# Attention and feed-forward on one core: two layer-one blocks to a bank, joined attention runs, a shorter state update

## The chip, the cores and the metric

The kernel runs on one core of a Trainium2 chip. The metric is the device time of one execution in microseconds, as the median of several runs. The profile is one execution; its span (first to last instruction) is 1.7 to 1.9 us shorter than the timed figure.

## The reference

Per batch and head, a gated linear attention: a 48 x 48 state decays by `alpha` at each of 768 steps, takes up the product of `k` and `v`, and is read by `q`. Its output, 3072 tokens of 384 features, goes through two dense layers with a tanh-gelu between.

```python
batch, n_heads, seq, head_dim = (4, 8, 768, 48)
for t in range(S):
    state = alpha[:, :, t, :, None] * state + einsum('bhd,bhe->bhde', k[:, :, t], v[:, :, t])
    y[:, :, t] = einsum('bhd,bhde->bhe', q[:, :, t], state)
x = y.transpose(0, 2, 1, 3).reshape(B * S, H * D)          # 3072 x 384
h = x @ w_in                                               # 384 -> 2048
g = 0.5 * h * (1 + tanh(c * (h + 0.044715 * h**3)))
out = g @ w_out                                            # 2048 -> 384
```

## The kernel before

The sequence is cut into six chunks of 128 tokens. A *unit* is one batch in one chunk, with eight heads; a *pair* is two units, and there are twelve pairs (0 to 11). For a pair, ACT forms exponentials of cumulative sums of log(alpha), DVE multiplies them into q and k (`qp`, `kp`), TensorE or a DMA turns these, TensorE forms the attention products `at` (k against q, 64 rows for each head), DVE masks them (`atm`), and TensorE forms y from them and from the state. y, turned, is the input of the two dense layers: layer one (`hT`), gelu on ACT (`gT`), layer two (`acc`). A small scheduler in the program, with a table of estimated costs `W`, decides the order in which all of this is recorded; on each engine the order is then fixed.

The eight accumulator banks of PSUM are given to three tags: `ca` (one buffer of two banks: cumulative sums, and one unit's attention products), `yk` (two of one bank), and `ff` (four of one bank: layer one, layer two, and in places attention products).

```python
BUFS = dict(ca=1, yk=2, ff=4, ...)

def attn(self, u, i):                       # one unit: 8 products of 64-row tiles
    ...
        if (u["m"], i) in self.AT_FF:
            at = [self.tile("ff", [C, H // 2, C], F32, "at") for _ in range(2)]
        else:
            at = self.tile("ca", [C, 2, H // 2, C], F32, "at")
            at = [at[:, 0], at[:, 1]]
        for p in range(H // 2):
            for o in range(2):
                sl = slice(64 * o, 64 * o + 64)
                nc.tensor.matmul(at[o][:, p, :], t[sl, 1, p, :], t[sl, 0, p, :], start=True, stop=True)

def carry(self, u, i, c, b):                # the state: four DVE operations of 64 partitions
    ...
        for o in range(2):
            ps, fs = slice(64 * o, 64 * o + 64), slice(D * o, D * o + D)
            acc = kv[ps, :, fs]
            if c > 0:
                s = self.sb.tile([C, H // 2, D], F32, tag=f"stmp{o}", bufs=2, name="stmp")
                nc.vector.tensor_tensor(s[ps], acc, old[ps, :, fs], op=ALU.add)
                acc = s[ps]
            nc.vector.tensor_tensor(new[ps, :, fs], acc, u["bend"][ps, i, :, None].to_broadcast(...), op=ALU.mult)

def layer1(self, f, c, lo, hi, nt):         # one block of 128 features for 256 tokens: half a bank
    ...
        h = f["h", c, lo, nt] = self.tile("ff", [self.C, (hi - lo) * self.C], F32, "hT")
        for j in range(self.NKT):           # 3 matmuls
            self.nc.tensor.matmul(h, ...)
def gelu(self, f, c, lo, hi, nt):           # one gelu a block
    ...
# ... (loads, exponentials, turns, y, layer two and the scheduler are cut)
```

Of the kernel before, what the change touches and what calls it, by code (L numbers as in the profile page):

```python
# [17 lines left out]
    qk2=910, qk1=500, ev8=650, ev4=350, mask=640, st=1400, st0=700, xc=520, xe=330, ot=540,  # L18
# [118 lines left out]
class _Kernel:  # L137
# [16 lines left out]
    AT_FF = ((0, 1),)  # L154

    URGENT = (2,)
    BUFS = dict(ca=1, yk=2, ff=4, la=3, qp=4, kp=4, b8=2, kn=2, qkT=4, atm=6, x=3, ot=6, bend=8,
                a=4, q=4, k=4, v=6)

    def __init__(self, ctx, tc, q, k, v, alpha, w_in, w_out, out):  # L160
# [25 lines left out]
        self.w_out = const.tile([C, self.NFT, self.d_model], BF16, name="w_out")  # L186
        self.state = [[const.tile([C, H // 2, 2 * D], BF16, name=f"st{b}_{i}") for i in range(2)]
# [222 lines left out]
    def attn(self, u, i):  # L410
        nc, H, C = self.nc, self.H, self.C

        def emit(e):
            t = u["T"][:, :, i]
            if (u["m"], i) in self.AT_FF:
                at = [self.tile("ff", [C, H // 2, C], F32, "at") for _ in range(2)]
            else:
                at = self.tile("ca", [C, 2, H // 2, C], F32, "at")
                at = [at[:, 0], at[:, 1]]
            u["at", i] = at  # L420
            for p in range(H // 2):
                for o in range(2):
                    sl = slice(64 * o, 64 * o + 64)
                    nc.tensor.matmul(at[o][:, p, :], t[sl, 1, p, :], t[sl, 0, p, :], start=True, stop=True)  # L424
        return emit
# [19 lines left out]

    def carry(self, u, i, c, b):
        nc, H, C, D = self.nc, self.H, self.C, self.D

        def emit(e):
            kv, old, new = u["kv", i], self.state[b][c % 2], self.state[b][(c + 1) % 2]  # L450
            for o in range(2):
                ps, fs = slice(64 * o, 64 * o + 64), slice(D * o, D * o + D)
                acc = kv[ps, :, fs]
                if c > 0:
                    s = self.sb.tile([C, H // 2, D], F32, tag=f"stmp{o}", bufs=2, name="stmp")
                    nc.vector.tensor_tensor(s[ps], acc, old[ps, :, fs], op=ALU.add)  # L456
                    acc = s[ps]
                nc.vector.tensor_tensor(new[ps, :, fs], acc,  # L458
                                        u["bend"][ps, i, :, None].to_broadcast([64, H // 2, D]), op=ALU.mult)
        return emit  # L460
# [32 lines left out]
    def layer1(self, f, c, lo, hi, nt):  # L493
        def emit(e):
            h = f["h", c, lo, nt] = self.tile("ff", [self.C, (hi - lo) * self.C], F32, "hT")
            for j in range(self.NKT):
                self.nc.tensor.matmul(h, self.w_in[:, j, nt * self.C:(nt + 1) * self.C],  # L497
                                      self.xT[c][:, j, lo:hi].rearrange("p g t -> p (g t)"),
                                      start=j == 0, stop=j == self.NKT - 1)
        return emit  # L500

    def gelu(self, f, c, lo, hi, nt):
        return lambda e: self.nc.scalar.activation(  # L503
            self.gT[c % self.NG][:, nt, lo * self.C:hi * self.C], f.pop(("h", c, lo, nt)), AF.Gelu_apprx_tanh)
# [32 lines left out]
    def tasks(self):  # L537
# [57 lines left out]
        for m, (c, i) in enumerate(pairs):  # L595
# [4 lines left out]
            lns[m], ends[m], qp, kp, be = [], [], [None, None], [None, None], [None, None]  # L600
            cums, exps = [], []
            for lo, hi in self.parts(m):
# [8 lines left out]
                if u["sums"]:  # L611
                    be[lo:hi] = [x[2]] * n
# [19 lines left out]
            vs, kvs, tq, cs, users = [], [], [], [], []  # L632
# [3 lines left out]
            if u["packed"]:  # L636
# [7 lines left out]
                owner = every[0]  # L644
            for j in range(2):
                b, o = 2 * i + j, P + 10 + 3 * j
                k = kp[j]
# [16 lines left out]
                at = s.add("attn", {"PE": W["attn"]}, o + 1, self.attn(u, j), turned)  # L664
                ms = [s.add("mask", {"DVE": W["mask"]}, o + 2, self.mask(u, j, h), [at]) for h in range(2)]
                if (m, j) in self.AT_FF:
                    at.take("ff", ms[0]).take("ff", ms[1])
                else:
                    at.take("ca", *ms)
# [12 lines left out]
                ats.setdefault(m, []).append(at)  # L682
# [3 lines left out]
                if c < NCH - 1:  # L686
                    if u["packed"]:
# [7 lines left out]
                                              [kv, be[j]] + ([states[b, c - 1], ys[b, c - 1]] if c else []))  # L695
# [12 lines left out]
            owner.take("qkT", *users)  # L708
# [3 lines left out]
            if u["sums"]:  # L712
                be[0].take("bend", *cs)


        n = 0
# [3 lines left out]
        def layer1(m):  # L720
# [4 lines left out]
            size = str(hi - lo)  # L725
            for nt in range(self.NFT):
                t = s.add("l1", {"PE": W["l1_" + size]}, 10000 + n, self.layer1(f, c, lo, hi, nt),
                          [xts[c, b] for b in range(lo, hi)] + [loads["w", "in", nt // 4]], stream=n)
                g = s.add("gelu", {"ACT": W["gelu" + size]}, 10000 + n, self.gelu(f, c, lo, hi, nt),
# [5 lines left out]
        def layer2(m):  # L735
# [4 lines left out]
            for u, part in ([(u, part) for part in parts for u in units] if m == 0 else [(u, part) for u in units for part in parts]):  # L740
                c, b = u
                t = s.add("l2", {"PE": W["l2"]}, 10000 + n, self.layer2(f, c, b, part),
                          gs[m if m else b // 2][4 * part:4 * part + 4] + [loads["w", "out", part]], stream=n)
# [27 lines left out]
    def run(self):  # L771
# [5 lines left out]
        make_identity(nc, self.ident)  # L777
        nc.vector.memset(self.blk, 0.0)  # L778
# [12 lines left out]
        for b in range(self.B):  # L791
            for i in range(2):
# [37 lines left out]
```

## Time and profile before

| | before |
|---|---|
| time, median of 4 | 184.94 us (184.51 to 185.05) |
| span of the profiled run | 183.2 us |
| busy: TensorE, ACT, DVE | 175.7, 135.6, 104.2 us |
| gelus | 192 of 387 ns |
| separate runs of attention products on TensorE | 23 |

In a row of the timeline, the first number is the start in us from the span's start, the second the length of the merged row, then engine, line, operation, output and input, shape, and count; brackets hold the idle time before it and what ended it. TensorE's matmuls overlap their tails, so its cost is read from start to start, not from the lengths.

I also use three stretches of TensorE's stream, measured from start to start of matmuls in the traces: from the span's start to the first layer-one matmul of the second block of 48 (before: 27.50 us), from there to the first of the third block (20.59 us), and from there to the last matmul (131.90 us).

### The profile page before, as it was taken

Reading aid. Unit: us, or ns where it says so; the run is one execution under the profiler, and the core shown is the slowest. Engines: PE = TensorE matmul, PEld = TensorE weight load, DVE = VectorE, ACT = ScalarE, POOL = GpSimd, SP = SyncE. Lnnn points to the kernel's source line nnn. Section 1 sums busy time; section 2 is a strip of 40 time slices with the busy share of each in tenths; the row PEclk is TensorE's granted clock in tenths of the full one; section 3 lists DMA queues with packets and bytes.
Section 4 is the critical chain, followed back from the end, with each engine's and each line's share of the span. In section 5 each row is a group of like instructions: output and inputs, shape, how many; then the busy total and the mean of one; then the engine's idle time right before and its main releaser. Section 6 shows DMA issues by size and latency. Waiting matters only on the chain.

```text
span 183.2 us, 4630 instructions
## 1 busy us (share of the span) xinstructions
PE 175.7 (96%) x1861; PEld 129.3 (71%) x1861; DVE 104.2 (57%) x232; ACT 135.6 (74%) x310; POOL 60.9 (33%) x68
## 2 busy tenths in 40 slices
PE   7887999999999999999999999999999999999993
PEld 2465869666686787687688769678677677686873
DVE  7775954065969896597499798298644715000000
ACT  3666969873888789859799768899789884491941
POOL 2595837975545755564750200000000000000000
PEclk9999999999999999999999999999999999999999
DMA  5999999999999999999999955753271290311102
GB/s 155 187 242 211 187 231 214 204 202 174 195 281 183 169 229 197 181 225 205 180 213 235 179 171 100 104 115 67 52 170 46 43 202 4 88 43 47 43 0 86
DMA packets 51206, 27.76 MB, mean 151 GB/s; under 512 B 38833, under 2 KB 48241, under 8 KB 51185
## 3 DMA queue, kind: packets, MB, share of 16 engines
q0 software_dynamic: 32096, 17.70, 69.0%
q1 hardware_dynamic: 18512, 9.38, 21.5%
q10 hardware_dynamic: 576, 0.39, 0.7%
q8 instruction: 14, 0.23, 0.6%
q14 instruction: 8, 0.06, 0.1%
HBM read 25.17 MB, written 4.72 MB: 163 GB/s over the span
## 4 chain that ended last, share of the span: by engine, by line
PE 85%; DMA 6%; ACT 3%; DVE 2%; SPq 1%; ACTq 1%; issue 0%
PE acc L516 34%; PE hT L497 31%; PE at L424 4%; PE qkT_ps L364 4%; PE yps L473 3%; DMA a<-in_alpha_dram 2%; PE yps L470 2%; DMA q<-in_q_dram 2%; PE cum L320 2%; PE kv L441 2%; DMA qkT<-kp 2%; PE xT_ps L487 1%; DVE atm L431 1%; ACT L503 1%; PE cum L322 1%; SPq L247 1%
## 5 line engine op out<-in xcount | busy, mean ns | idle before, releaser
L497 PE MATMUL hT<-xT,w_in 128*128 128x256 bf16 x576 | 70.1, 273 | 0.4 <-ACT gT L503 0.4
L503 ACT ACTIVATE gT<-hT 128x256 bf16<-128x256 f32 x192 | 63.4, 387 | 8.6 <-PE hT L497 8.3
L516 PE MATMUL acc<-w_out,gT 128*128 128x384 bf16 (+1 forms) x400 | 68.8, 319 | 0.0
L497 PEld LDWEIGHTS <-w_in 128*128 128x128 bf16 x576 | 54.0, 98 | 8.0 <-issue 0.6
L516 PEld LDWEIGHTS <-gT 128*128 128x128 bf16 x400 | 36.8, 98 | 19.6
L431 DVE TENSOR_TENSOR atm<-at,ut 128x512 bf16<-128x512 f32 x48 | 30.9, 685 | 15.0 <-PE at L424 14.5
L354 DVE TENSOR_TENSOR qp<-q,b 128x768 bf16<-128x768 f32 (+1 forms) x15 | 11.7, 794 | 18.7 <-ACT b L343 15.8
L528 ACT COPY ot<-acc 128x384 f32<-128x384 f32 (+1 forms) x18 | 8.3, 462 | 13.9 <-PE acc L516 12.6
L235 POOL DMA_DIRECT2D v<-in_v_dram x13 | 14.6, 1123 | 9.6 <-PE hT L497 2.9
L235 POOL DMA_DIRECT2D k<-in_k_dram x11 | 12.2, 1112 | 11.0 <-DVE kp L354 5.2
L343 ACT ACTIVATE b<-cum 128x768 bf16<-128x768 f32 (+1 forms) x15 | 10.2, 684 | 6.7 <-PE cum L322 3.1
L235 POOL DMA_DIRECT2D q<-in_q_dram x11 | 12.3, 1114 | 7.0 <-DMA k<-in_k_dram 1.8
L235 POOL DMA_DIRECT2D a<-in_alpha_dram x11 | 12.3, 1114 | 5.9 <-ACT gT L503 2.2
L213 ACT ACT_TABLE_LOAD x9 | 11.5, 1283 | 2.8 <-issue 2.6
L480 ACT CAST x<-yps 128x384 bf16<-128x384 f32 x16 | 7.7, 481 | 7.8 <-PE yps L473 7.6
L458 DVE TENSOR_TENSOR st<-stmp,bend 64x192 bf16<-64x192 f32 x32 | 11.3, 353 | 1.5
L354 DVE TENSOR_TENSOR kp<-k,binv 128x768 bf16<-128x768 f32 (+1 forms) x15 | 11.8, 792 | 0.2
L456 DVE TENSOR_TENSOR stmp<-kv,st 64x192 f32<-64x192 f32 x32 | 11.3, 352 | 1.0 <-PE kv L441 0.7
L503 ACT ACT_TABLE_LOAD x9 | 11.5, 1283 | 0.2
L222 PE MATMUL idle<-zero 128*128 128x512 bf16 x27 | 9.5, 462 | 1.2 <-DVE blk L778 1.2
L382 DVE COPY qkT<-qkT_ps 128x1024 bf16<-128x1024 bf16 (+1 forms) x13 | 8.7, 688 | 3.0 <-PE qkT_ps L364 2.9
L343 ACT ACTIVATE binv<-cum 128x768 bf16<-128x768 f32 (+1 forms) x15 | 10.1, 683 | 0.0
(62 smaller groups left out, 159.4 us busy)
## 6 DMA issues: line engine op xcount, KB each, us to landing
out_dram<-ot SPq DMA_DIRECT2D x23, 192.0 KB, 2.3
a<-in_alpha_dram POOLq DMA_DIRECT2D x9, 384.0 KB, 13.1
q<-in_q_dram POOLq DMA_DIRECT2D x9, 384.0 KB, 13.2
k<-in_k_dram POOLq DMA_DIRECT2D x9, 384.0 KB, 13.3
v<-in_v_dram POOLq DMA_DIRECT2D x11, 192.0 KB, 13.3
w_in<-in_moe_w_in_dram POOLq DMA_DIRECT2D x4, 384.0 KB, 7.7
w_out<-in_moe_w_out_dram POOLq DMA_DIRECT2D x4, 384.0 KB, 9.8
a<-in_alpha_dram SPq DMA_DIRECT2D x6, 96.0 KB, 3.4
```

The source lines that it names most:

```text
L213: nc.scalar.add_instruction(mybir.InstLoadActFuncSet(name=nc.get_next_instruction_name(), act_func_set_id=i, engine=mybir.EngineType.Activ ...
L222: self.nc.tensor.matmul(ps, self.zero[:, 0:self.C], self.zero, start=True, stop=True)
L235: (nc.sync if e == "SP" else nc.gpsimd).dma_start(u[n][:, lo:hi].rearrange("t b h d -> t (b h) d"), src)
L343: self.nc.scalar.activation(u[n].rearrange("t i h d -> t i (h d)")[:, lo:hi], cum, AF.Exp, scale=1.0 if n == "b" else -1.0)
L354: self.nc.vector.tensor_tensor(out, rows, b, op=ALU.mult)
L382: self.copy(e)(t, ps)
L431: self.nc.vector.tensor_tensor(u["atm", i][:, o], u["at", i][o], self.ut[:, None, :].to_broadcast([self.C, self.H // 2, self.C]), op=ALU.mult)
L456: nc.vector.tensor_tensor(s[ps], acc, old[ps, :, fs], op=ALU.add)
L458: nc.vector.tensor_tensor(new[ps, :, fs], acc, u["bend"][ps, i, :, None].to_broadcast([64, H // 2, D]), op=ALU.mult)
L497: self.nc.tensor.matmul(h, self.w_in[:, j, nt * self.C:(nt + 1) * self.C], self.xT[c][:, j, lo:hi].rearrange("p g t -> p (g t)"), start=j ...
L503: return lambda e: self.nc.scalar.activation(self.gT[c % self.NG][:, nt, lo * self.C:hi * self.C], f.pop(("h", c, lo, nt)), AF.Gelu_apprx_ ...
L516: self.nc.tensor.matmul(f["acc", c, b][:, lo:hi], self.gT[c % self.NG][:, nt, b * self.C:(b + 1) * self.C], self.w_out[:, nt, lo:hi], star ...
```

## The change

Three things. **(G)** Two layer-one blocks share a bank, and one gelu takes both. **(A)** For pairs 3 to 11, the attention products of both units stand in one run; the first unit's go to two `ff` banks, the second's to `ca`. **(S)** The state's update takes two operations of 128 partitions, with a factor `ends` that is zero off the two heads' blocks, so the states need no clearing at the start. The table of costs is changed to fit, so the program orders itself anew. The core of the diff:

```diff
-    AT_FF = ((0, 1),)
+    AT_FF, SINGLE = {0: (1,), 1: (), 2: ()}, (0, 1, 2)
 ... (cut)
-    def attn(self, u, i):
+    def attn(self, u, units, apart):
         nc, H, C = self.nc, self.H, self.C
 
         def emit(e):
-            t = u["T"][:, :, i]
-            if (u["m"], i) in self.AT_FF:
-                at = [self.tile("ff", [C, H // 2, C], F32, "at") for _ in range(2)]
-            else:
-                at = self.tile("ca", [C, 2, H // 2, C], F32, "at")
-                at = [at[:, 0], at[:, 1]]
-            u["at", i] = at
-            for p in range(H // 2):
-                for o in range(2):
-                    sl = slice(64 * o, 64 * o + 64)
-                    nc.tensor.matmul(at[o][:, p, :], t[sl, 1, p, :], t[sl, 0, p, :], start=True, stop=True)
+            for i in units:
+                if i in apart:
+                    u["at", i] = [self.tile("ff", [C, H // 2, C], F32, "at") for _ in range(2)]
+                else:
+                    at = self.tile("ca", [C, 2, H // 2, C], F32, "at")
+                    u["at", i] = [at[:, 0], at[:, 1]]
+            for i in units:
+                t, at = u["T"][:, :, i], u["at", i]
+                for p in range(H // 2):
+                    for o in range(2):
+                        sl = slice(64 * o, 64 * o + 64)
+                        nc.tensor.matmul(at[o][:, p, :], t[sl, 1, p, :], t[sl, 0, p, :], start=True, stop=True)
         return emit
 ... (cut)
+    def ends(self, u):
+        C, H = self.C, self.H
+
+        def emit(e):
+            t = u["ends"] = self.tile("ends", [C, 2, H // 2, 2], F32)
+            self.nc.vector.tensor_tensor(
+                t.rearrange("f i p o -> f (i p) o"), u["bend"].rearrange("f i p -> f (i p)")[:, :, None].to_broadcast([C, H, 2]),
+                self.half[:, None, :].to_broadcast([C, H, 2]), op=ALU.mult)
+        return emit
+
     def carry(self, u, i, c, b):
         nc, H, C, D = self.nc, self.H, self.C, self.D
 
         def emit(e):
-            kv, old, new = u["kv", i], self.state[b][c % 2], self.state[b][(c + 1) % 2]
-            for o in range(2):
-                ps, fs = slice(64 * o, 64 * o + 64), slice(D * o, D * o + D)
-                acc = kv[ps, :, fs]
-                if c > 0:
-                    s = self.sb.tile([C, H // 2, D], F32, tag=f"stmp{o}", bufs=2, name="stmp")
-                    nc.vector.tensor_tensor(s[ps], acc, old[ps, :, fs], op=ALU.add)
-                    acc = s[ps]
-                nc.vector.tensor_tensor(new[ps, :, fs], acc,
-                                        u["bend"][ps, i, :, None].to_broadcast([64, H // 2, D]), op=ALU.mult)
+            acc, old, new = u["kv", i], self.state[b][c % 2], self.state[b][(c + 1) % 2]
+            if c > 0:
+                s = self.sb.tile([C, H // 2, 2 * D], F32, tag="stmp", bufs=2, name="stmp")
+                nc.vector.tensor_tensor(s, acc, old, op=ALU.add)
+                acc = s
+            ends = u["ends"][:, i].rearrange("f p o -> f (p o)")[:, :, None].to_broadcast([C, H, D])
+            nc.vector.tensor_tensor(new.rearrange("f p (o d) -> f (p o) d", o=2),
+                                    acc.rearrange("f p (o d) -> f (p o) d", o=2), ends, op=ALU.mult)
         return emit
 ... (cut)
     def layer1(self, f, c, lo, hi, nt):
         def emit(e):
-            h = f["h", c, lo, nt] = self.tile("ff", [self.C, (hi - lo) * self.C], F32, "hT")
-            for j in range(self.NKT):
-                self.nc.tensor.matmul(h, self.w_in[:, j, nt * self.C:(nt + 1) * self.C],
-                                      self.xT[c][:, j, lo:hi].rearrange("p g t -> p (g t)"),
-                                      start=j == 0, stop=j == self.NKT - 1)
+            h = f["h", c, lo, nt] = self.tile("ff", [self.C, 2, (hi - lo) * self.C], F32, "hT")
+            for s in range(2):
+                for j in range(self.NKT):
+                    self.nc.tensor.matmul(h[:, s], self.w_in[:, j, (nt + s) * self.C:(nt + s + 1) * self.C],
+                                          self.xT[c][:, j, lo:hi].rearrange("p g t -> p (g t)"),
+                                          start=j == 0, stop=j == self.NKT - 1, skip_group_check=True)
         return emit
 
     def gelu(self, f, c, lo, hi, nt):
         return lambda e: self.nc.scalar.activation(
-            self.gT[c % self.NG][:, nt, lo * self.C:hi * self.C], f.pop(("h", c, lo, nt)), AF.Gelu_apprx_tanh)
+            self.gT[c % self.NG][:, nt:nt + 2, lo * self.C:hi * self.C], f.pop(("h", c, lo, nt)), AF.Gelu_apprx_tanh)
 ... (cut: costs, buffers of bend and ends, and the tasks that follow from these)
-        for b in range(self.B):
-            for i in range(2):
-                nc.vector.memset(self.state[b][i], 0.0)
```

More of the change, by code (lines that the diff above doesn't have):

```diff
@@ L17 @@
     cum=530, cum_packed=1500, t8=450, t4=225, attn=340, kv=170, inter=170, intra=205, tx=168, l1_4=655, l1_2=340, l2=655,
-    qk2=910, qk1=500, ev8=650, ev4=350, mask=640, st=1400, st0=700, xc=520, xe=330, ot=540,
+    qk2=910, qk1=500, ev8=650, ev4=350, mask=640, st=1090, st0=545, end=110, attn2=590, xc=520, xe=330, ot=540,
     ev8_act=960, ev4_act=520, xc_act=450, xe_act=450, ot_act=450,
@@ L152 @@
     EV_ACT = (0, 1, 2, 3)
-    AT_FF = ((0, 1),)
+    AT_FF, SINGLE = {0: (1,), 1: (), 2: ()}, (0, 1, 2)
     URGENT = (2,)
-    BUFS = dict(ca=1, yk=2, ff=4, la=3, qp=4, kp=4, b8=2, kn=2, qkT=4, atm=6, x=3, ot=6, bend=8,
+    BUFS = dict(ca=1, yk=2, ff=4, la=3, qp=4, kp=4, b8=2, kn=2, qkT=4, atm=6, x=3, ot=6, bend=3, ends=8,
                 a=4, q=4, k=4, v=6)
@@ L186, in __init__ @@
         self.w_out = const.tile([C, self.NFT, self.d_model], BF16, name="w_out")
+        self.half = const.tile([C, 2], F32, name="half")
         self.state = [[const.tile([C, H // 2, 2 * D], BF16, name=f"st{b}_{i}") for i in range(2)]
@@ L599, in tasks @@
             early = m in self.EARLY
-            lns[m], ends[m], qp, kp, be = [], [], [None, None], [None, None], [None, None]
+            lns[m], ends[m], qp, kp, be = [], [], [None, None], [None, None], []
             cums, exps = [], []
@@ L611, in tasks @@
                 if u["sums"]:
-                    be[lo:hi] = [x[2]] * n
+                    be.append(x[2])
                 ends[m].append(x[-1])
@@ L631, in tasks @@
             exps[0].take("b8", *qp, *kp)
-            vs, kvs, tq, cs, users = [], [], [], [], []
+            vs, kvs, tq, cs, users, turns, masks = [], [], [], [], [], [], {}
             if m in self.TURN_QK:
@@ L644, in tasks @@
                 owner = every[0]
+            if u["sums"]:
+                end = s.add("end", {"DVE": W["end"]}, P + 16, self.ends(u), be)
             for j in range(2):
-                b, o = 2 * i + j, P + 10 + 3 * j
-                k = kp[j]
+                o, k = P + 10 + 3 * j, kp[j]
                 if u["packed"]:
@@ L663, in tasks @@
                             owner = turned[0]
-                at = s.add("attn", {"PE": W["attn"]}, o + 1, self.attn(u, j), turned)
-                ms = [s.add("mask", {"DVE": W["mask"]}, o + 2, self.mask(u, j, h), [at]) for h in range(2)]
-                if (m, j) in self.AT_FF:
-                    at.take("ff", ms[0]).take("ff", ms[1])
-                else:
-                    at.take("ca", *ms)
+                turns.append(turned)
+                if m in self.SINGLE or j:
+                    units = (j,) if m in self.SINGLE else (0, 1)
+                    apart = self.AT_FF.get(m, (0,))
+                    at = s.add("attn", {"PE": W["attn" if len(units) == 1 else "attn2"]}, o + 1, self.attn(u, units, apart), sum(turns[units[0]:], []))
+                    ats.setdefault(m, []).append(at)
+                    for w in units:
+                        ms = masks[w] = [s.add("mask", {"DVE": W["mask"]}, P + 12 + 3 * w, self.mask(u, w, h), [at]) for h in range(2)]
+                        if w in apart:
+                            at.take("ff", ms[0]).take("ff", ms[1])
+                        else:
+                            at.take("ca", *ms)
+            for j in range(2):
+                b, o, k, ms, turned = 2 * i + j, P + 10 + 3 * j, kp[j], masks[j], turns[j]
+                at = ats[m][-1 if m not in self.SINGLE else j]
                 y = s.add("y", {"PE": W["intra"] + (W["inter"] if c else 0)}, P + 20 + j, self.y(u, j, c, b),
@@ L681, in tasks @@
                 users += [at, y]
-                ats.setdefault(m, []).append(at)
                 ms[0].take("atm", y)
@@ L694, in tasks @@
                     st = states[b, c] = s.add("st", {"DVE": W["st" if c else "st0"]}, P + 30 + j, self.carry(u, j, c, b),
-                                              [kv, be[j]] + ([states[b, c - 1], ys[b, c - 1]] if c else []))
+                                              [kv, end] + ([states[b, c - 1], ys[b, c - 1]] if c else []))
                     kv.take("yk", st)
@@ L707, in tasks @@
                     t.deps += [xts[c, 2 * i], xts[c, 2 * i + 1]]
-            owner.take("qkT", *users)
+            owner.take("qkT", *dict.fromkeys(users))
             qp[0].take("qp", *tq)
@@ L712, in tasks @@
             if u["sums"]:
-                be[0].take("bend", *cs)
+                be[0].take("bend", end)
+                end.take("ends", *cs)
         n = 0
@@ L724, in layer1 @@
             lo, hi = 2 * pairs[ps[0]][1], 2 * pairs[ps[-1]][1] + 2
-            size = str(hi - lo)
-            for nt in range(self.NFT):
-                t = s.add("l1", {"PE": W["l1_" + size]}, 10000 + n, self.layer1(f, c, lo, hi, nt),
+            for nt in range(0, self.NFT, 2):
+                t = s.add("l1", {"PE": W["l1_4"]}, 10000 + n, self.layer1(f, c, lo, hi, nt),
                           [xts[c, b] for b in range(lo, hi)] + [loads["w", "in", nt // 4]], stream=n)
-                g = s.add("gelu", {"ACT": W["gelu" + size]}, 10000 + n, self.gelu(f, c, lo, hi, nt),
+                g = s.add("gelu", {"ACT": W["gelu4"]}, 10000 + n, self.gelu(f, c, lo, hi, nt),
                           [t] + between[m - 1] + (l2s.get(c - self.NG, []) if nt == 0 else gs[m][:1]), GELU)
@@ L742, in layer2 @@
                 t = s.add("l2", {"PE": W["l2"]}, 10000 + n, self.layer2(f, c, b, part),
-                          gs[m if m else b // 2][4 * part:4 * part + 4] + [loads["w", "out", part]], stream=n)
+                          gs[m if m else b // 2][2 * part:2 * part + 2] + [loads["w", "out", part]], stream=n)
                 l2s.setdefault(c, []).append(t)
@@ L777, in run @@
         make_identity(nc, self.ident)
+        nc.vector.memset(self.half, 0.0)
+        for o in range(2):
+            nc.vector.memset(self.half[64 * o:64 * o + 64, o:o + 1], 1.0)
         nc.vector.memset(self.blk, 0.0)
```

## The prediction

> **What bounds the kernel now.** I read the busy line and the slices of the page first, then the chain that ended last, then the groups with the idle time before them, and last the TensorE timeline around single events.
>
> ```profile
> PE 175.7 (96%) x1861; PEld 129.3 (71%) x1861; DVE 104.2 (57%) x232; ACT 135.6 (74%) x310; POOL 60.9 (33%) x68
> PE   7887999999999999999999999999999999999993
> ACT  3666969873888789859799768899789884491941
> PE 85%; DMA 6%; ACT 3%; DVE 2%; SPq 1%; ACTq 1%; issue 0%
> L497 PE MATMUL hT<-xT,w_in 128*128 128x256 bf16 x576 | 70.1, 273 | 0.4 <-ACT gT L503 0.4
> L503 ACT ACTIVATE gT<-hT 128x256 bf16<-128x256 f32 x192 | 63.4, 387 | 8.6 <-PE hT L497 8.3
> ```
>
> TensorE is busy in 96% of the span and, from the fifth slice (about 18 us) to the last, in nine tenths or more of each. The chain is TensorE for 85%. ACT waits for TensorE (8.3 us ahead of the gelus), not the other way round: all the layer-one matmuls together lost 0.4 us to a gelu. So work taken from ACT or DVE is worth only what it takes out of a TensorE wait, while time taken out of TensorE's own stream is worth its full size. The granted clock is 0.999 over the span, so nothing is to be had there.
>
> "Busy" does not mean streaming. The rates come from undisturbed stretches of the chain: 48 layer-one matmuls in 5.24 us, or 0.109 us each; 32 layer-two matmuls in 5.20 us, or 0.163 us each. With these I read the timeline of TensorE around one attention run and around the one visible wait (columns: start, length, line, tile, shape, count):
>
> ```profile
> 63.69 0.82 PE L497 MATMUL hT<-xT,w_in 128*128 128x256 bf16 x6
> 64.44 0.40 PE L424 MATMUL at<-qkT 64*128 64x128 bf16 x8
> 64.77 0.51 PE L441 MATMUL kv<-v,kp 128*128 128x96 bf16 x8
> ...
> 10.64 0.66 PE L424 MATMUL at<-qkT 64*128 64x128 bf16 x16
> ...
> 48.09 1.47 PE L497 MATMUL hT<-xT,w_in 128*128 128x256 bf16 x12
> 48.23 1.28 ACT L503 ACT_TABLE_LOAD   x1
> 49.96 0.27 PE L497 MATMUL hT<-xT,w_in 128*128 128x256 bf16 x1 [0.40 <-ACT gT L503]
> ```
>
> First group: six matmuls from 63.69 should be through at 63.69 + 6 x 0.109 = 64.34; the attention products (64-row tiles) start at 64.44, and the next 128-row work at 64.77. So a run of 8 holds TensorE for 64.77 - 64.34 = 0.43 us. Second: the one run of 16 takes 0.66 us against 0.40 us for 8, both with the same tail, so 8 more products inside a run cost about 0.25 us by these rounded lengths, and 0.22 us by the spacing of the products' starts (8 starts from 64.44, four pairs some 0.055 us apart). I use 0.23 us. Hence a run costs about **0.20 us** beyond its products, for going into 64-row tiles and out again. Third: 12 matmuls from 48.09 should end at 49.40, and the next starts at 49.96, after the first gelu behind the table load: a wait of 0.56 us.
>
> **What the Trainium skill says.** "TensorEngine Tiling (Array Packing)", Key Properties: changing the tiling mode drains TensorE. The trace agrees: 0.20 us a round trip, as above. "ScalarE: Activation LUTs", Table sets: an ACTIVATE without pointer operands takes 186 ns + 0.833 ns an element, and neighbours overlap by about 93 ns. The trace has 387 ns for 256 elements (the formula gives 399), and a row of 7 gelus in 2.30 us, so one every (2.30 - 0.387) / 6 = 0.319 us. "PSUM — Partial Sum Buffer", Specifications: a bank holds 512 fp32 values per partition; a layer-one block of 256 tokens thus used half of its buffer. "VectorE: DVE Perf Modes", The TRN2 errata: an fp32 tensor_tensor takes (N + 151) / 0.96 ns. The trace agrees: 681 ns by its median for the masks of 512 columns (formula 691), 352 ns for the state's operations of 192 (357).
>
> **The change part by part.**
>
> *Two blocks in a bank, one gelu.* TensorE's 576 matmuls stay. 192 gelus become 96. By slope, 256 more elements at 0.833 ns add 0.213 us, so one of 512 is issued every 0.319 + 0.213 = 0.532 us in place of 0.638 us for two: 96 x 0.106 = 10.2 us less on ACT, but ACT is not the bound. More to the point, the four buffers now hold 24 matmuls (2.6 us of TensorE) where they held 12 (1.3 us). A table load of 1.28 us and the first gelu (48.23 to about 50.13 us) then fit beneath the 2.6 us. That removes the 0.56 us, and probably a second layer-one wait of 0.13 us that the starts show at 108.3 us: **0.7 us**. It holds only if the next thing behind these matmuls, the turning of k, is ready earlier too: kp's multiply ends at 52.5 us, after qp and eight state operations. With four of the new ones, below, it ends near 51.7 us, and TensorE would arrive near 51.9 us. It just fits.
>
> *Attention products in one run.* Before, the trace has 23 separate runs (pair 0's two stand together). The order of the changed program has pairs 0 to 2 as they were and one run of 16 for each of pairs 3 to 11, so 14. Nine round trips less x 0.20 us, all on the path: **1.8 us**. Besides, two of the old runs waited longer, 0.09 us at 122 us and 0.19 us at 150.7 us, the latter for a DMA turn of kp that landed at 151.08. In the new order the run at that place stands behind 42 layer-one matmuls instead of 36, or 0.65 us later: **0.2 us** more.
>
> *State in two operations.* For 16 units with an old state: four operations of 0.352 us become two of 128x384. Length by the slope between 192 and 512 columns, (681 - 352) / 320 = 1.03 ns: 0.352 + 192 x 1.03 = 0.55 us. So 1.41 becomes 1.10 us, -5.0 us in all; the four first units -0.16 us each; eight memsets of the states -1.7 us; ten small multiplies (ends) of about 0.11 us each +1.1 us. DVE falls by some 6 us of 104, nearly all off the path. The memsets end at 6.0 us while the first multiply waits until 7.4 us for b and data. One place lies on the path: at 21.4 us two state operations (0.72 us) stand ahead of the masks that the next attention run waits for; one of 0.55 us gives **0.15 us**.
>
> Sum: 0.7 + 1.8 + 0.2 + 0.15 = 2.85 us. I take off 0.35 us for small waits that a new order of this size usually makes, so 2.5 us: 184.9 - 2.5 = **182.4 us**.
>
> **The rivals.**
> 1. *New waits eat the gain.* A pair's attention run now takes two of the four buffers at once, until two masks are through, and all four masks (4 x 0.65 us) stand in a row, with y behind. For: there are only two or three buffers left for layer one and acc. Against: the new order puts 12 to 18 layer-one matmuls (1.3 to 2 us) between the run and the first y, or 6 layer-one and 8 layer-two (0.65 + 1.3 us) in the last pairs; masks of the first unit should be ready about 1.3 us after the run's end. Slack of a few tenths each. If it fails by 0.2 us in each of nine pairs, 184.2 us.
> 2. *The freed engines pay in full.* ACT -10 us, DVE -6 us. For: ACT at 74% and, in the layer-one stretches, as slow as TensorE (16 x 0.319 = 5.1 us against 5.24 us). Against: from 30 us on, TensorE's waits outside the attention runs add up to about 1.1 us, so there is nothing more to win: 181.5 us at the most.
> 3. *Only the early part decides.* Before 30 us TensorE waits about 7 us and runs 27 idle matmuls. There the order before and after is almost the same, those 27 stay in the program, and what they wait for (loads, ln, exp, the first turns) is untouched. Hence not more than the 0.15 us above.
> 4. *DMA.* It is busy in nine tenths of the slices until about 105 us, but loads ended little of ACT's or DVE's idle time there, as buffers are loaded well ahead. Hidden in both.
>
> **Range and chances.** The firm part is 1.8 us; all waits that I can see removed would give about 3.3 us; rival 1 at its worst would leave about 0.7 us. Adding 0.3 us for the scatter of runs (184.51 to 185.05), I take 181.4 to 183.8 us. Faster by over 2% means below 181.24 us, more than the waits that I found: 0.07. Slower by over 2% would need a serious new wait: 0.02. Within 2%: 0.91.
>
> **What would show it.** Right, if: TensorE busy is near 173 to 174 us; the gelus number 96 at about 0.60 us, ACT near 125 us, DVE near 98 us; attention rows show 9 runs of 16 that take about 0.65 us from the preceding matmul's end to the next 128-row start; the wait for gT ahead of hT is gone or under 0.1 us; layer one still 0.109 us each. The span falls by as much as TensorE's waits do, not by the 16 us taken from ACT and DVE. Wrong, if: hT waits for atm (the two buffers), y's weight loads wait for atm, turns of k wait for kp behind ends, each some tenths at several pairs; or if a run of 16 costs as much as two of 8; or if the start, up to 30 us, shifts by over half a us.

## The result, and the profile after

The changed kernel takes 181.88 us (median of 4, 181.34 to 182.27) against 184.94 us: 3.06 us less by the medians. The ratio, which here and below is the mean time of one kernel's fast runs over that of the other's of the same rounds, is 0.9839, with a 95% interval of 0.9807 to 0.9871. That is within 2%, and clear of noise.

First the page of the changed kernel: busy time, the chain by engine, and the two groups of layer one.

```profile
PE 172.8 (96%) x1858; PEld 130.1 (72%) x1861; DVE 96.9 (54%) x201; ACT 129.8 (72%) x214; POOL 61.1 (34%) x68
PE 87%; DMA 8%; POOL 2%; ACT 1%; SPq 1%; issue 0%; POOLq 0%
L508 PE MATMUL hT<-xT,w_in 128*128 128x256 bf16 x576 | 69.5, 273 | 0.2 <-DMA w_in<-in_moe_w_in_dram 0.2
L514 ACT ACTIVATE gT<-hT 128x512 bf16<-128x512 f32 x96 | 56.7, 597 | 16.6 <-PE hT L508 13.3
```

The span fell by 2.7 us, and TensorE's busy time by 2.9 us on this page. That second figure is partly an accident of the records: this profile shows 24 idle matmuls (on zeros, into a buffer that nothing reads), the profile before 27, and a second profile of the changed kernel again 27, with TensorE busy for 174.1 us, only 1.6 us less than before. So the busy total is a rough measure here; the stretches from start to start, below, show that the gain is in TensorE's stream, as the chain (87% TensorE) would have it. The gelus are 96 of 597 ns, and layer one no longer waits for a gelu; the 0.2 us that it still waits are for a load of weights in the start-up. ACT fell by 5.8 us and DVE by 7.3 us, 13 us together, which did not come out of the span.

The timeline around the attention run that answers to the one at 64.44 us before:

```profile
63.93 0.82 PE L508 MATMUL hT<-xT,w_in 128*128 128x256 bf16 x6
64.13 0.56 DVE L465 TENSOR_TENSOR stmp<-kv,st 128x384 f32<-128x384 f32 x1
64.68 0.62 PE L426 MATMUL at<-qkT 64*128 64x128 bf16 x16
64.72 0.56 DVE L468 TENSOR_TENSOR st<-stmp,ends 128x384 bf16<-128x384 f32 x1
65.20 2.48 DVE L433 TENSOR_TENSOR atm<-at,ut 128x512 bf16<-128x512 f32 x4
65.23 0.34 PE L443 MATMUL kv<-v,kp 128*128 128x96 bf16 x4
65.41 2.13 PE L508 MATMUL hT<-xT,w_in 128*128 128x256 bf16 x18
```

Six layer-one matmuls from 63.93 end at 63.93 + 6 x 0.109 = 64.58; the run of 16 starts at 64.68 and the next 128-row work at 65.23. It holds TensorE for 0.65 us, where two runs of 8 held it for 2 x 0.43 us. DVE has only two state operations to do ahead of the masks (65.20), and layer one goes on for 18 matmuls from 65.41 with no wait.

The place of the 0.56 us wait before:

```profile
48.27 4.09 PE L508 MATMUL hT<-xT,w_in 128*128 128x256 bf16 x36
48.41 1.28 ACT L514 ACT_TABLE_LOAD   x1
49.71 3.29 ACT L514 ACTIVATE gT<-hT 128x512 bf16<-128x512 f32 x6
50.81 0.95 DVE L355 TENSOR_TENSOR kp<-k,binv 128x768 bf16<-128x768 f32 x1
52.42 0.39 PE L365 MATMUL qkT_ps<-ident,kp 128*128 128x128 bf16 x4
```

All 36 matmuls run through while ACT loads its table, and k's multiply (50.81 + 0.95 = 51.76) is done before its turn at 52.42. The promised order of events holds, with 0.66 us to spare.

One new wait is in the stretch before that:

```profile
35.57 0.32 PE L321 MATMUL cum<-la,ut_h 128*128 128x384 f16 x1
36.01 0.49 ACT L344 ACTIVATE b<-cum 128x384 bf16<-128x384 f32 x1
36.40 0.48 ACT L344 ACTIVATE binv<-cum 128x384 bf16<-128x384 f32 x1
36.93 0.32 PE L321 MATMUL cum<-la,ut_h 128*128 128x384 f16 x1 [0.29 <-ACT binv L344]
```

The second cumulative sum of pair 2 waits for the first unit's exponential, `binv`, on ACT. By the spacing of the starts that costs 0.45 us. In the order before, both sums stood side by side ahead of the exponentials.

The stretches say the same: the third is 129.00 us (2.90 us less), the second 20.97 us (0.38 us more), the first 27.31 us (within its own scatter). The two that repeat thus give 2.52 us; what the medians show beyond that (3.06 us here, 2.66 us in the control below) lies in the start and the scatter of the runs.

### The profile page after: what moved, and what is told of

Its sections match the earlier page's. It is cut to its first block, busy times and chain, and to the rows that moved or that the text cites. A ratio compares the mean times of both kernels' runs of the same rounds, so it can differ in the third digit from the quotient of the medians.

```text
span 180.5 us, 4489 instructions
## 1 busy us (share of the span) xinstructions
PE 172.8 (96%) x1858; PEld 130.1 (72%) x1861; DVE 96.9 (54%) x201; ACT 129.8 (72%) x214; POOL 61.1 (34%) x68
## 4 chain that ended last, share of the span: by engine, by line
PE 87%; DMA 8%; POOL 2%; ACT 1%; SPq 1%; issue 0%; POOLq 0%
PE hT L508 35%; PE acc L527 34%; DMA w_in<-in_moe_w_in_dram 5%; PE at L426 4%; PE qkT_ps L365 3%; PE yps L483 3%; PE kv L443 2%; PE cum L321 2%; PE yps L480 2%; DMA k<-in_k_dram 2%; DMA a<-in_alpha_dram 1%; PE xT_ps L497 1%; POOL k L248 1%; PE cum L323 1%; SPq L248 1%; PE idle L223 1%
## 5 line engine op out<-in xcount | busy, mean ns | idle before, releaser
L514 ACT ACTIVATE gT<-hT 128x512 bf16<-128x512 f32 x96 | 56.7, 597 | 16.6 <-PE hT L508 13.3
L433 DVE TENSOR_TENSOR atm<-at,ut 128x512 bf16<-128x512 f32 x48 | 30.0, 683 | 13.5 <-PE at L426 13.5
L490 ACT CAST x<-yps 128x384 bf16<-128x384 f32 x15 | 7.2, 479 | 5.3 <-PE yps L483 5.2
L383 DVE COPY qkT<-qkT_ps 128x1024 bf16<-128x1024 bf16 (+1 forms) x12 | 7.9, 687 | 3.9 <-PE qkT_ps L365 3.8
L223 PE MATMUL idle<-zero 128*128 128x512 bf16 x24 | 8.6, 450 | 1.3 <-DVE half L798 1.2
L465 DVE TENSOR_TENSOR stmp<-kv,st 128x384 f32<-128x384 f32 x16 | 8.8, 551 | 1.2 <-PE kv L443 1.2
L468 DVE TENSOR_TENSOR st<-stmp,ends 128x384 bf16<-128x384 f32 x16 | 8.9, 558 | 0.6
```

The lines of the kernel that those rows point to most:

```text
L223: self.nc.tensor.matmul(ps, self.zero[:, 0:self.C], self.zero, start=True, stop=True)
L433: self.nc.vector.tensor_tensor(u["atm", i][:, o], u["at", i][o], self.ut[:, None, :].to_broadcast([self.C, self.H // 2, self.C]), op=ALU.mult)
L465: nc.vector.tensor_tensor(s, acc, old, op=ALU.add)
L468: nc.vector.tensor_tensor(new.rearrange("f p (o d) -> f (p o) d", o=2), acc.rearrange("f p (o d) -> f (p o) d", o=2), ends, op=ALU.mult)
L514: return lambda e: self.nc.scalar.activation(self.gT[c % self.NG][:, nt:nt + 2, lo * self.C:hi * self.C], f.pop(("h", c, lo, nt)), AF.Gelu ...
```

## The experiments

The theory after the result: TensorE's stream is the bound; the nine saved round trips into 64-row tiles (about 1.9 us) and the removed waits (about 1 us) are the gain; ACT's and DVE's lighter load counts only where TensorE waits for it. The rivals: the lighter ACT or DVE pays by itself; the new order pays; or the parts need one another. Twelve kernels were run in three groups of four, all correct.

### 1. The changed kernel again (control)

No edit.

> The changed kernel itself, unaltered, as the control of this group. Both theories: 0.984 of the kernel before (181.9 us against 184.9), its profiled span near 180.5 us, nine attention runs of 16, and again one wait of about 0.45 us of the second cumulative sum near 36 us for the exponential on ACT.

Measured: 182.19 us, ratio 0.9849 (0.9816 to 0.9882); third stretch 129.00 us, second 20.96 us. It repeats.

### 2. The joined runs broken again, in the same order

```diff
-            for i in units:
-                ... products of unit i
+            products(units[0])
+            self.later = [(u["m"], i, products) for i in units[1:]]
 ... (in run(), where the tasks are recorded)
             t.emit(t.engine)
+            if t.engine == "PE" and t.kind != "attn":
+                for m, i, products in self.later:
+                    products(i)
+                self.later = []
```

> The changed kernel with each of the nine runs of 16 attention products broken in two by the one TensorE task that stands behind it anyway; same instructions, same order otherwise. Theory (going into 64-row tiles and out again costs 0.20 us of TensorE's own stream each time): 9 x 0.20 = 1.8 us slower than the control, so about 183.7 us, with 23 attention runs, and about 0.19 us more at each of nine places, no other wait grown. Rival (the gain of the change comes from other waits, the order or the lighter ACT and DVE): within 0.4 us of the control.

The timeline of TensorE at the same pair:

```profile
64.25 0.40 PE L419 MATMUL at<-qkT 64*128 64x128 bf16 x8
64.58 0.34 PE L446 MATMUL kv<-v,kp 128*128 128x96 bf16 x4
64.85 0.40 PE L419 MATMUL at<-qkT 64*128 64x128 bf16 x8
```

The four kv products (0.17 us by their starts) now stand between two runs of 8; of the 0.27 us from 64.58 to 64.85, 0.10 us is the way into the 64-row tiles a second time. From 64.25 to 64.58 is a run of 8 until other work starts, 0.33 us, of which 0.11 us beyond the products' 0.22 us is the way out. Measured: 183.89 us, ratio 0.9941 (0.9904 to 0.9978), which is 1.7 us slower than the control by the medians. The third stretch is 130.92 us, 1.92 us more than the control's, or 0.21 us for each of nine places, with no other wait grown over 0.1 us. The theory's 1.8 us holds; the rival's "within 0.4 us" does not. Going into 64-row tiles and out again is a cost of TensorE's own stream.

### 3. ACT's load given back

```diff
             ... gelu ...
+            self.nc.scalar.copy(self.junk[:, 0:32], self.zero[:, 0:32])
```

> The changed kernel with a small copy on ACT behind each of the 96 gelus (32 columns into a tile that nothing reads), about 0.12 us each, so that ACT carries again the 10 us of which the change relieved it; the buffers and the order of all other work are as in the changed kernel. Theory (ACT's busy time is worth nothing, only waits of TensorE are): within 0.4 us of the control, at most 182.3 us. Rival (the lighter ACT pays by itself): 1 us or more slower, with TensorE waiting for gelus ahead of layer one or layer two.

The groups of ACT, gelus and the added copies (`junk`):

```profile
L516 ACT ACTIVATE gT<-hT 128x512 bf16<-128x512 f32 x96 | 57.4, 599 | 11.2 <-PE hT L509 10.8
L518 ACT COPY junk<-zero 128x32 bf16<-128x32 bf16 x96 | 20.3, 212 | 0.0
```

A copy takes 0.21 us, not the 0.12 us expected, but overlaps its neighbours. ACT is busy for 136.6 us, more than the 135.6 us of the kernel before. Measured: 182.06 us, ratio 0.9847 (0.9815 to 0.9879); third stretch 129.12 us, 0.12 us more than the control's. ACT's time is worth next to nothing here: 6.8 us of it for 0.12 us. The rival's 1 us or more is refuted.

### 4. and 5. Each of the other two ways to the same end: joined runs alone, pairs of blocks alone

Joined runs alone, on the kernel before:

```diff
-    AT_FF = ((0, 1),)
+    AT_FF, SINGLE = {0: (1,), 1: (), 2: ()}, (0, 1, 2)
 ... (attn and its tasks as in the change; layer1, gelu, carry as before)
```

> The kernel before with the attention runs joined alone; the program's own ordering follows from it. Theory: nine round trips less at 0.20 us and the two longer waits of attention runs (0.09 and 0.19 us) gone: 1.8 to 2.1 us faster than before, about 182.9 us, with the 0.56 us wait for the first gelu near 49 us still there. Rival (the three parts need each other): less than 1 us faster.

Measured: 187.13 us against 185.43 us in this group, ratio 1.0096 (1.0050 to 1.0142): **slower**. Theory and rival both said faster; both are refuted in their sign, though the rival's idea that the parts need each other is on the right side. TensorE's stream is 1.72 us longer in the third stretch, although 1.9 us of round trips are saved: 3.6 us of new waits. Two places of the timeline show which:

```profile
80.56 0.62 PE L425 MATMUL at<-qkT 64*128 64x128 bf16 x16
80.79 0.35 DVE L459 TENSOR_TENSOR st<-stmp,bend 64x192 bf16<-64x192 f32 x1
81.16 0.36 DVE L457 TENSOR_TENSOR stmp<-kv,st 64x192 f32<-64x192 f32 x1
81.29 0.82 PE L498 MATMUL hT<-xT,w_in 128*128 128x256 bf16 x6
81.94 1.89 DVE L432 TENSOR_TENSOR atm<-at,ut 128x512 bf16<-128x512 f32 x3
82.68 0.49 PE L498 MATMUL hT<-xT,w_in 128*128 128x256 bf16 x3 [0.57 <-DVE atm L432]
```

The run of 16 takes two of the four `ff` buffers. Layer one puts six matmuls (81.29) into the other two, since a block of 256 tokens takes a whole buffer for half a bank; then it waits until 82.68 for the first mask to give a buffer back. That mask stands at 81.94, behind state operations (80.79, 81.16, and one more at 81.55).

```profile
94.87 0.23 PE L425 MATMUL at<-qkT 64*128 64x128 bf16 x1
95.15 0.94 ACT L504 ACTIVATE gT<-hT 128x256 bf16<-128x256 f32 x3
95.59 0.60 PE L425 MATMUL at<-qkT 64*128 64x128 bf16 x15 [0.49 <-ACT gT L504]
```

Here the first product of a run is out, and the second waits until the gelu behind a table load gives back the buffer that it needs.

Pairs of blocks alone, on the kernel before:

```diff
-            h = f["h", c, lo, nt] = self.tile("ff", [self.C, (hi - lo) * self.C], F32, "hT")
+            h = f["h", c, lo, nt] = self.tile("ff", [self.C, 2, (hi - lo) * self.C], F32, "hT")
 ... (layer1, gelu and their tasks as in the change; attn, carry as before)
```

> The kernel before with two blocks in a bank and one gelu alone. Theory: the layer-one waits of 0.56 and 0.13 us go, but the new order puts four layer-two matmuls between pair 2's two sums, as in the changed kernel, which costs some 0.4 us; net 0.2 to 0.5 us faster than before, about 184.5 us, though ACT is some 10 us lighter. Rival (ACT's 10 us pay): 1 us or more faster.

Measured: 185.40 us against 185.43 us, ratio 1.0006 (0.9962 to 1.0050). The third stretch is 0.34 us shorter, the second 0.38 us longer (the wait of pair 2's second sum, 0.45 us, is there): together nothing. The expected 0.2 to 0.5 us are not seen by the time. In the third stretch the waits for gelus went, but 0.63 us of a new wait came in at 62.9 us, where a turn of q waits for a copy of xT that stands behind `kp` on DVE. The rival (1 us or more from the lighter ACT) is refuted once more.

### 6. The state update alone

On the kernel before:

```diff
-st=1400, st0=700
+st=1090, st0=545, end=110
 ... (ends, carry, their buffers and tasks, no clearing of the states, as in the change; attn, layer1, gelu as before)
```

> The kernel before with the state's update in two operations alone. Theory: DVE about 6 us lighter, TensorE's stream the same, so within 0.4 us of before (gain 0 to 0.3 us), with the 0.56 us wait near 49 us still there. Rival (DVE's time pays): 1 us or more faster.

Measured: 185.49 us against 185.43 us, ratio 0.9995 (0.9957 to 1.0032), as the theory had it: DVE's busy time is 5 us less and buys nothing. The third stretch is even 0.90 us longer; in the order that follows from it, layer one waits for gelus 0.34 us near 109 us and 0.78 us near 123 us, with half-used buffers as before. The rival (1 us or more faster) is refuted.

### 7. Four state operations in the changed kernel, same order

```diff
-                nc.vector.tensor_tensor(s, acc, old, op=ALU.add)
+                nc.vector.tensor_tensor(s[ps], acc, old[ps, :, fs], op=ALU.add)      # twice, o = 0, 1
 ...
+                nc.vector.tensor_tensor(new[ps, :, fs], acc, u["ends"][ps, i, :, o:o + 1].to_broadcast(...), op=ALU.mult)
 ... (and the states cleared at the start, as before)
```

> The changed kernel, same order on TensorE, ACT, SP and GpSimd, with each state's update again in four operations of 64 partitions. Theory (the state part is worth only what it keeps ready for TensorE at one place): k's multiply ends about 0.9 us later near 52 us, and TensorE waits some 0.3 to 0.5 us ahead of its turns there; otherwise hidden, so 0.3 to 0.6 us slower than the changed kernel, about 182.4 us. Rival (nothing waits for the state): within 0.15 us of it and no new wait near 52 us.

Measured: ratio 0.9878 (0.9842 to 0.9914), 183.39 us; the third stretch is 130.38 us, 1.38 us more than the changed kernel's. The expected wait near 52 us is there (0.34 us by the starts), but it is only a quarter of the loss. The rest are waits that I had not expected, as at this pair (to be held against the lines at 64 us above):

```profile
65.38 0.62 PE L426 MATMUL at<-qkT 64*128 64x128 bf16 x16
65.58 0.36 DVE L468 TENSOR_TENSOR stmp<-kv,st 64x192 f32<-64x192 f32 x1
65.97 0.35 DVE L470 TENSOR_TENSOR st<-stmp,ends 64x192 bf16<-64x192 f32 x1
66.11 0.82 PE L510 MATMUL hT<-xT,w_in 128*128 128x256 bf16 x6
66.36 1.89 DVE L433 TENSOR_TENSOR atm<-at,ut 128x512 bf16<-128x512 f32 x3
67.10 1.14 PE L510 MATMUL hT<-xT,w_in 128*128 128x256 bf16 x9 [0.17 <-DVE atm L433]
```

Four state operations where two stood push the first mask to 66.36, about 1.0 us after the run's start against 0.5 us; layer one gets six matmuls in and then waits until 67.10 for the buffer. The same happens at 95.4 us, and a y waits for its mask at 108.6 us (0.32 us). The theory was right in the mechanism and too small by more than half; the rival is refuted.

### 8. to 10. Each part left out of the changed kernel

Without G, on the changed kernel:

```diff
-            h = f["h", c, lo, nt] = self.tile("ff", [self.C, 2, (hi - lo) * self.C], F32, "hT")
+            h = f["h", c, lo, nt] = self.tile("ff", [self.C, (hi - lo) * self.C], F32, "hT")
 ... (layer1, gelu and their tasks as before)
```

> The changed kernel without the pairing of layer-one blocks (joined attention runs and the state in two operations stay). Theory A (the joined run takes two of four buffers, and only with two blocks in a buffer is there room for TensorE to go on): little or nothing left of the gain, within 1 us of before, with waits of layer one or of attention products for buffers that add up to 1 us or more. Rival B (the joined runs alone failed because DVE's four state operations held up the masks; the state part cures that): 1.5 us or more faster than before.

Measured: 185.08 us against 185.15 us, ratio 0.9998 (0.9969 to 1.0028). Theory A holds and rival B fails: nothing left of the gain, with 0.69 us of a product waiting for a gelu's buffer, and layer one waiting 0.56 us at the old place.

Without S, on the changed kernel:

```diff
-st=1090, st0=545, end=110
+st=1400, st0=700
 ... (carry and its tasks as before)
```

> The changed kernel without the state part (joined attention runs and paired blocks stay; the program orders itself anew). Theory A (buffers matter most, DVE's time second, as the run with four operations in the changed order showed 1.2 us of new waits): 1 to 2 us faster than before. Rival B (DVE's time is what the joined runs need): less than 0.5 us faster than before.

Measured: 185.92 us against 185.15 us, ratio 1.0058 (1.0024 to 1.0093). Theory A, 1 to 2 us faster, fails; rival B's "less than 0.5 us faster" is on the right side, though it did not say that the kernel would be slower. Some of it is chance of the start (the profiled run had 29.2 us in the first stretch), but the third stretch, 132.15 us, alone shows 3.15 us lost against the changed kernel. The waits of TensorE that the profile names:

```profile
PE at L425 <- DMA qkT<-kp: 1.0, 1, 1.0
PE hT L499 <- DVE atm L432: 0.7, 3, 0.2
```

Layer one waits for masks, and one run of products waits 1.0 us for a DMA turn of kp (1.15 us by the starts). The changed kernel has no such wait; whether DVE's longer operations or the other order bring it was not separated.

Without A, on the changed kernel:

```diff
-    AT_FF, SINGLE = {0: (1,), 1: (), 2: ()}, (0, 1, 2)
+    AT_FF = ((0, 1),)
 ... (attn and its tasks as before)
```

> The changed kernel without the joining of attention runs (paired blocks and the state part stay). Theory: 23 runs again, so some 1.8 to 2.0 us slower than the changed kernel, 0.5 to 1.1 us faster than before, with few waits on TensorE beyond the 0.2 us at each run. Rival (the two other parts make the gain): 1.5 us or more faster than before.

Measured: 183.90 us against 185.15 us, ratio 0.9921 (0.9891 to 0.9950), third stretch 130.94 us, 1.94 us more than with A. The time alone does not part the theory (0.5 to 1.1 us faster than before) from the rival (1.5 us or more), as the interval reaches from 0.9 to 2.0 us; the stretches do: the third is 0.96 us shorter than before and the second 0.38 us longer, together 0.58 us. So the theory holds, and agrees with experiment 2 to 0.02 us, though the order is another.

All eight combinations, by the third stretch (us) and the ratio to the kernel before:

| parts | third stretch | ratio |
|---|---|---|
| none | 131.90 | 1 |
| G | 131.56 | 1.0006 |
| A | 133.62 | 1.0096 |
| S | 132.80 | 0.9995 |
| A + S | 132.53 | 0.9998 |
| G + A | 132.15 | 1.0058 |
| G + S | 130.94 | 0.9921 |
| G + A + S | 129.00 | 0.9839 |

Joining the runs costs 1.7 us alone, 0.6 us with G, gains 0.3 us with S, and 1.9 us with both.

### 11. and 12. The new wait taken away

First, the second sum recorded ahead of the first unit's exponentials, with the order of every engine unchanged.

> The changed kernel, with the second cumulative sum of pair 2 recorded ahead of the first unit's exponentials instead of between them; the order of the instructions on every engine is the same. Theory (the sum waited because the two units' sums lie in one tile, and recording them in the other order removes that dependency): the wait of about 0.45 us near 36 us is gone and the time falls by 0.3 to 0.45 us against the control, to about 181.5 us. Rival (what it feeds, exponentials, multiplies and turns, keeps TensorE waiting as long a little later): wait gone, time within 0.15 us of the control.

```diff
+        late = [t for t in order[:n] if t.kind in ("b", "binv", "bend") and t.at == (2, 0)]
+        order = [t for t in order[:n] if t not in late] + [second] + late + order[n + 1:]
```

Measured: 181.52 us, ratio 0.9822 (0.9784 to 0.9860). The 0.45 us wait is gone, so it came from the order of recording and not from data; but 0.23 us appear in a turn of k at 38.1 us, since the exponentials now wait for the later sum. Of the second stretch's 0.38 us, 0.18 us are back (20.79 us), between the theory's 0.3 to 0.45 us and the rival's 0.15 us; the medians (181.52 against the control's 182.19 us) scatter too much to tell.

Then the sum moved directly behind the first on TensorE too.

> The changed kernel with the second cumulative sum of pair 2 directly behind the first on TensorE and in the program, as in the kernel before, all else the same. Theory: the wait of 0.45 us near 36 us goes and no other takes its place (the earlier try left 0.23 us in a turn of k, since both exponentials then waited for the later sum): 0.3 to 0.45 us faster than the changed kernel, 0.982 of before. Rival (the wait only moves): within 0.15 us of the changed kernel in the stretch from 27 to 48 us.

```diff
+        first, second = [t for t in order if t.kind == "cum" and t.at[0] == 2]
+        order.remove(second)
+        order.insert(order.index(first) + 1, second)
```

```profile
35.59 0.32 PE L321 MATMUL cum<-la,ut_h 128*128 128x384 f16 x1
36.01 0.32 PE L321 MATMUL cum<-la,ut_h 128*128 128x384 f16 x1
36.27 2.11 PE L527 MATMUL acc<-w_out,gT 128*128 128x384 bf16 x12
36.45 0.49 ACT L344 ACTIVATE b<-cum 128x384 bf16<-128x384 f32 x1 [0.49 <-PE cum L323]
```

The second sum starts 0.42 us after the first, layer two follows at once, and the exponentials have both sums. Measured: 181.79 us against 185.15 us, ratio 0.9813 (0.9779 to 0.9847); second stretch 20.67 us, 0.30 us less than the changed kernel's, third stretch the same 129.01 us. The theory's 0.3 us is just reached, and the rival's 0.15 us exceeded. It is the shortest kernel by the two stretches, by 0.3 us against the changed kernel and 0.1 us against experiment 11; the timed intervals of it and of the changed kernel (0.9839, 0.9849) overlap, so the times alone don't show it.

## Why the prediction was right, and where it was not

The prediction said 182.4 us (181.4 to 183.8) and within 2%; it was 181.88 us. Its net 2.5 us are what the two repeating stretches show (2.52 us), and its large terms agree one by one, as follows, so the sum is not luck, though the 0.35 us taken off was a guess that named no place. The upper end of the range is less well founded: the worst case told for rival 1 was 184.2 us, beyond the 183.8 us of the range.

**TensorE bounds the kernel, so only its stream counts.** Right for the sum: 2.7 us of span went, of 13 us taken from ACT and DVE; ACT's load given back cost 0.12 us (experiment 3).

**Nine round trips at 0.20 us, 1.8 us.** Right: 1.92 us and 1.94 us in two experiments, 0.21 us each.

**The wait for the first gelu, 0.7 us, and two longer waits of attention runs, 0.2 us.** Right: none of them is in the new trace, and 1.92 + 0.69 + 0.28 is 2.89 us of the third stretch's 2.90 us. The condition that kp be ready also held, at 51.76 us against the 51.7 us told.

**The state part is worth 0.15 us, as DVE is off the path.** This step failed as a statement on the part. In the kernel before it is right (alone, nothing). In the changed kernel it is worth 1.4 us in the same order and 3.2 us in the order that the program makes without it, because joined runs hold two buffers until DVE has masked them, and DVE's queue has the state operations ahead of the masks. The sum came out since the waits were read in the new order with all three parts in place; the split of it over the parts did not. The same holds for "1.8 us, all on the path": true given G and S, and of the wrong sign alone. Rival 1, new waits for the two buffers, was the true danger; the prediction gave it "slack of a few tenths each", and experiments 4, 7, 8 and 9 show that G and S are where that slack comes from.

**0.35 us off for small new waits.** The size was right (0.38 us in the second stretch). The prediction did not know where: a sum that waits for an exponential of the other unit.

**The start gives nothing but 0.15 us.** Not resolved. The wait of an attention run near 23 us fell by 0.29 us by the starts, but the first stretch scatters by more than that.

**Busy times.** DVE 96.9 us (told: 98). ACT 129.8 us (told: 125): gelus that wait for TensorE no longer overlap, so that each adds its full 0.59 us, not 0.53 us. Here the prediction misread its row of seven gelus: five of the six spacings from 68.79 us are 0.327 us, the time of three layer-one matmuls (3 x 0.109), so the 0.319 us is TensorE's pace and not ACT's. Where results lay ready, behind the table load at 48.23 us, gelus of 256 started 0.264 to 0.280 us apart. At 0.27 us, 16 gelus take an estimated 4.3 us against TensorE's 5.24 us, so ACT was not "as slow as TensorE" there, and rival 2 had less for it than told. The small `ends` take 0.16 to 0.17 us each, not 0.11 us; by the formula that the prediction quotes from the skill, the estimate is (16 + 151) / 0.96 = 174 ns, which would have been the better source.

**Small slips that change nothing.** The last slice of TensorE's row is at 3 tenths, not at nine or more. The formula for an ACTIVATE stands in the page's section What ACT_TABLE_LOAD costs, not in the one that the prediction named.

What stays open: how much of the orders' differences (experiments 4 to 6 and 8 to 10 change the order along with the part) belongs to the part and how much to the order; experiments 2 (but for one task at each of nine places), 3, 7 and 11 keep the order and don't have this doubt.

## What to carry to other kernels

When one engine's stream is the bound, count what a change takes out of that stream and out of its waits; busy time of the other engines was worth nothing here except where a buffer that the bound engine needed waited for them. Price each part in the order and with the buffers of the finished change: joining work into longer runs holds more buffers for longer, and may need another part, which gains nothing by itself, to make room. When a scheduler orders the program, test a part by keeping the order and changing that part alone.

## What the Trainium skill lacked or had wrong

- "TensorEngine Tiling (Array Packing)", Key Properties, says that changing the tiling mode drains TensorE, without a size. Here going from 128-row to 64-row tiles and back costs 0.21 us (1.92 us for nine), about 0.1 us each way.
- "ScalarE: Activation LUTs", What ACT_TABLE_LOAD costs: neighbours are said to overlap by about 93 ns. Where their results lay ready, the overlap here was larger: behind a table load, gelus of 256 elements (from 49.53 us before) started 264 to 280 ns apart and overlapped by 104 to 151 ns, and the first four of 512 (from 49.71 us after) 477 to 494 ns apart, by 104 to 127 ns. The formula for one (186 ns + 0.833 ns an element) gives estimates of 399 and 612 ns where the traces have 387 and 597 ns.
- "VectorE: DVE Perf Modes", The TRN2 errata: the page checks (N + 151) / 0.96 ns at 512 and 2048 columns. Here it also agrees, within some 10 ns, at 384 (estimate 557 ns against 551 to 558 ns) and at 16 columns (174 ns against 162 to 170 ns).
- No page that I read tells that two results in different banks of one tile can make one wait for readers of the other: here a cumulative sum waited 0.45 us for an exponential of the other half of its tile, and recording it earlier, with every engine's order unchanged, took that wait away. That the shared tile is the reason was not tested apart from the order of recording.
